# Decoder tables of a neural codec kernel: from scaled adds on ScalarE and VectorE to diagonal matmuls in PSUM

## The chip, the cores and the metric

The kernel runs on one core of a Trainium2 chip. The metric is the device time of one execution in microseconds. The engines are called PE (TensorE, matmuls), DVE (VectorE), ACT (ScalarE), POOL (GpSimd) and SP (SyncE, which only issues transfers here).

## The reference

The input x has shape (2, 16000, 512). A depthwise convolution of three taps along time, followed by SiLU, gives z. Four codebooks of eight vectors then quantise z one after another: each stage takes the nearest codebook vector and subtracts it. The sum of the chosen vectors goes through a second depthwise convolution of three taps.

```python
z = jnp.zeros_like(x)
for i in range(K):
    z = z + xp[:, i:i+T, :] * dw_enc[i][None, None, :]
z = _silu(z)
res = z
q = jnp.zeros_like(z)
for s in range(Nq):
    cb = codebooks[s]
    d2 = |res|^2 - 2.0 * res @ cb.T + |cb|^2
    sel = cb[d2.argmin(-1)]
    q = q + sel
    res = res - sel
for i in range(K):
    y = y + qp[:, i:i+T, :] * dw_dec[i][None, None, :]
```

All arrays are bf16; K is 3, Nq is 4, and the d2 line is shortened here.

## The kernel before

Each of the two sequences is cut into nine tiles, eighteen in all: the first sequence into 6, 8 and seven times 16 groups of 128 rows, the second into seven times 16, 8 and 6. A tile's rows are loaded transposed (channels on partitions) by DMA transposes from SP, one per group, into one of two XT buffers.

For each tile the steps are these. `front` makes the three taps (the "taps" steps, L531 on ACT or L532 on DVE, and adds through the helper at L364), then the exponential (L537) and one plus it (L538 or L539). `front2` takes the reciprocal (L549) and multiplies ("gate"). `select` computes inner products with codebooks on PE (L561, L567, "score0"), reads them on DVE (L601, L602), and decides the first three stages with small DVE steps ("decide"), small transposes copied to OT (L643 on ACT, L644 on DVE) and corrections on PE (L649). `windows` transposes the one-hot choices (L672) and copies them to OHW (L678, either engine). `resid` subtracts the chosen vectors: PE multiplies OHW by the negated codebook tables CBN (L701, with L700 adding Z through an identity where ACT evacuates), and ACT (L707) or DVE (L709) brings the result back to ZB. A second round of products and decisions (`score3`, `decide3`, `win3`) settles the last stage. `back` multiplies OHW by the decoder tables WDEC on PE (L758, L760, L762), ACT copies the result to YB (L766), and SP stores it (L789).

Because one one-hot window covers four neighbouring rows for every stage, a decoder table has 128 rows (stage, row offset jj, codeword) by 512 channels: row r holds the codebook vector (in CB4) times the decoder tap that belongs to the row offset jj of r. There are four tables WDEC[v]; v says which taps stand at which offsets, in `(0, 1, 2, None), (None, 0, 1, 2), (None, None, 0, None), (None, 2, None, None)`. JM[jj] is a column of ones and zeros that marks the partitions of offset jj. WDBC holds the three decoder taps, each repeated on all partitions; it lives in YB3, and the scratch rows WJ live in YB2. The negated stage tables CBN are made from CB4 in the same setup, and CB4 is copied from PSUM by ACT (L458).

In the kernel before, each table is a sum of terms tap times mask, made by ACT (L481) and added on DVE, and then one product with CB4 on DVE:

```python
add("ACT", 0.62, key, lambda t=t, k=k, jj=jj: nc.scalar.mul(t, WDBC[:, k, :], JM[jj]), [("Y", 3), ("JM", jj)], [("WJ", jj % 2)])
if acc is not None:
    tt(t, t, acc, ALU.add, 0.35, key, [("WJ", 1 - jj % 2)], [("WJ", jj % 2)])
...
tt(WDEC[v], CB4, acc, ALU.mult, 0.35, key, ["CB4", ("WJ", aj), ("Y", 3)], [("WDEC", v), ("Y", 2)])
```

The order of all instructions is made by a planner, class `Plan`. Every step is added with an engine, an assumed cost, a key and its dependences. `order` then replays the steps on assumed clocks: it always takes the step that can start earliest, and among equals the one of least rank. The rank comes from a table WHEN with three entries for each kind of step (the first three tiles, the middle, the last three). Steps that may run on two engines go to ACT only if it would end early enough by SLACK; evacuations of `resid` choose by SHARE. Where PE would idle long before a step that is not setup, the planner puts in filler matmuls (L809). The engines then execute their own instructions strictly in that order. Setup steps and the first tiles' steps are planned together, so setup work can lie between the first tiles' work.

Of the kernel before, what the change touches and what calls it, by code (L numbers as in the profile page):

```python
# [8 lines left out]
BF16 = mybir.dt.bfloat16  # L9
F32 = mybir.dt.float32  # L10
U16 = mybir.dt.uint16
ALU = mybir.AluOpType
# [4 lines left out]
class Plan:  # L17
# [9 lines left out]
    SPAN, BUSY = 3.413, 0.5  # L27
    GATE = {"resid": (1.0, 2.0), "back": (1.0, 2.0), "win0": (0.6, 1.5), "win3": (0.6, 1.5), "score0": (0.25, 1.4), "score3": (0.25, 1.4)}

    def __init__(self, pairs, edges, share, slack, quota, when):  # L30
        self.steps, self.writer, self.readers = [], {}, {}
        self.pairs, self.edges, self.share, self.slack, self.quota, self.when = pairs, edges, share, slack, quota, when

    def add(self, engine, cost, key, fn, reads=(), writes=(), take=None, free=None, hold=None, tail=0.0, after=(), dest=None, box=None, mm=0):
        n = len(self.steps)
        deps = set(after)
        for t in reads:
            if t in self.writer:
                deps.add(self.writer[t])
            self.readers.setdefault(t, []).append(n)  # L40
        for t in writes:
            if t in self.writer:
                deps.add(self.writer[t])
            deps.update(self.readers.get(t, ()))
            self.writer[t] = n
            self.readers[t] = []
        deps.discard(n)
        self.steps.append({"n": n, "e": engine, "c": cost, "k": key, "fn": fn, "deps": sorted(deps), "take": take, "free": free,
                           "hold": hold, "tail": tail, "dest": dest, "box": box, "mm": mm})
        return n  # L50
# [3 lines left out]

    def rank(self, s):
        w = self.when[s["k"][0]][self.part(s)]
        return w[0] + s["k"][1] + w[1] * s["k"][2]

    def product(self, t, c, share, half):

# [14 lines left out]
    def order(self):  # L75
# [17 lines left out]
        out = []  # L93
# [9 lines left out]
        def load(d, t):  # L103
            return max(clock[d] - t, 0.0) + held[d] + sum(cost(steps[m], d) for m in waiting[d]
                                                        if at[m] <= t + 1.0 and (d == "DVE" or not isinstance(steps[m]["e"], tuple)))
# [8 lines left out]
        def look(s, e):  # L114

            t = max(at[s["n"]], clock[e])
            if s["take"]:
                dest = s["dest"]
                if dest == "ANY":
                    full = [d for d in ("ACT", "DVE") if held[d] >= self.quota[d]]  # L120
                    if len(full) == 2:
                        return inf, None
                    if full:
                        dest = "ACT" if full[0] == "DVE" else "DVE"
                    else:
                        dest = "DVE" if load("DVE", t) + self.share[self.part(s)] < load("ACT", t) else "ACT"
                elif dest and held[dest] >= self.quota[dest]:
                    return inf, None
                kind = s["take"][0]
                t = place(kind[dest] if isinstance(kind, dict) else kind, t)[0]  # L130
                return t + late(many(s, dest), t, cost(s, dest) if s["dest"] == "ANY" else s["c"]), dest
            if isinstance(s["e"], tuple) and e == "ACT" and t + s["c"]["ACT"] > max(at[s["n"]], clock["DVE"]) + s["c"]["DVE"] + self.slack[self.part(s)]:
                return inf, None
            if s["mm"]:
                t += late(s["mm"], t, s["c"])
            return t, None
# [9 lines left out]
        while len(out) < len(steps):  # L146
# [38 lines left out]
                c += self.TABLE  # L185
            if s["mm"]:
                m = many(s, dest)
                c = self.product(t, c, *self.GATE.get(s["k"][0], (0.5, 1.5))) - t
                run += m
                if run > self.CHUNK:  # L190
                    run -= self.CHUNK
                    fetched = t + c * (m - run) / m + self.FETCH
# [4 lines left out]
            if s["free"]:  # L197
                if s["free"]["dest"]:
                    held[s["free"]["dest"]] -= 1
                for j in s["free"]["banks"]:  # L200
                    banks[j] = end + self.LATENCY[e]
            out.append(s)
            for u in users[n]:
                ue = steps[u]["e"]
                at[u] = max(at[u], t + c + self.AGAIN[e] if ue == e else end + self.LATENCY[e])
                left[u] -= 1
                if not left[u]:
                    open_(u)
# [5 lines left out]
def kernel(  # L214
# [27 lines left out]
    PAIR = 1  # L242
    NX, NE, NZ, NOH, NY = 2, 3, 4, 4, 4
    NA = 4
    SHARE = (19.5, 1.71, -1.34)
    SLACK = (0.8, -4.83, -5.72)
    QUOTA = {"ACT": 4, "DVE": 4}
    WHEN = {"setup": ((-0.05, 1.675), (0.613, 1.016), (0.464, 0.931)), "load": ((-2.074, 0.741), (-2.063, 0.601), (-2.58, 0.741)),
            "pad": ((-1.343, 0.11), (-1.736, 0.115), (-2.291, 0.134)), "taps": ((0.284, 0.643), (-0.413, 0.648), (0.441, 1.172)),
            "exp": ((0.672, 0.139), (0.624, 0.043), (0.853, 0)), "plus1": ((1.287, 0.521), (0.349, 0.234), (0.268, 0.646)),  # L250
            "recip": ((0.542, 0.819), (0.469, 0.213), (1.361, 0.627)), "gate": ((-0.104, 0.712), (0.552, 0.521), (1.523, 0.809)),
            "score0": ((-0.134, 0), (0.889, 0), (-0.19, 0)), "decide": ((1.83, 0.266), (-0.088, 0.293), (0.366, 0.69)),
            "win0": ((2.039, 0), (2.077, 0), (2.756, 0)), "resid": ((1.585, 0.742), (1.683, 0.632), (1.826, 0.993)),
            "score3": ((2.285, 1.086), (2.738, 0.327), (2.939, 1.624)), "decide3": ((1.327, 0.17), (2.815, 0.429), (3.624, 0.724)),
            "win3": ((3.135, 0.143), (3.003, 1.197), (2.818, 0.209)), "back": ((2.723, 0.576), (3.156, 1.159), (4.372, 0.628))}
    assert B == len(SIZES) and T >= GM * P and GM <= 16

    xf = x.flatten_outer_dims()
# [63 lines left out]
    CBN = {(s, u): sb([P, D], BF16, f"CBN{s}_{u}") for s in range(3) for u in range(2)}  # L322
    WDEC = [sb([P, D], BF16, f"WDEC{v}") for v in range(4)]

    plan = Plan(NA, (3, len(tiles) - 3), SHARE, SLACK, QUOTA, WHEN)
    add = plan.add

    def ps(box):
# [37 lines left out]
    def setup():  # L366
# [104 lines left out]
                       ["CB4", ("JN", u)], [("CBN", s, u)])  # L471

        key = ("setup", 2.3, 0)
        WJ = [YB[2][:, j, :] for j in range(2)]
        for v, tp in enumerate(((0, 1, 2, None), (None, 0, 1, 2), (None, None, 0, None), (None, 2, None, None))):
            acc = None
            for jj, k in enumerate(tp):
                if k is None:
                    continue
                t = WJ[jj % 2]  # L480
                add("ACT", 0.62, key, lambda t=t, k=k, jj=jj: nc.scalar.mul(t, WDBC[:, k, :], JM[jj]), [("Y", 3), ("JM", jj)], [("WJ", jj % 2)])  # L481
                if acc is not None:
                    tt(t, t, acc, ALU.add, 0.35, key, [("WJ", 1 - jj % 2)], [("WJ", jj % 2)])
                acc, aj = t, jj % 2
            tt(WDEC[v], CB4, acc, ALU.mult, 0.35, key, ["CB4", ("WJ", aj), ("Y", 3)], [("WDEC", v), ("Y", 2)])

    def load(st):
        n, G = st["n"], st["G"]
# [358 lines left out]
```

## Time and profile before

| quantity | value |
|---|---|
| median of 7 runs | 731.39 us (726.59 to 733.28) |
| profiled execution, its own time | 732.25 us |
| its span | 730.5 us |
| mean granted TensorE clock | 0.963 |
| time in the setup's eight ACT multiplies (L481) | 5.6 us in total |
| DMA, mean | 98 GB/s |

The span is the time from the first to the last recorded instruction of the profiled execution; its own time includes what lies around it. A row of a group names line, engine, operation, output and inputs with their shapes, how often, then the busy time in us and the mean of one in ns, then the idle time of the engine just before it and who ended it. Busy shares are averages over stages, so a table by stage is needed beside them.

### The profile page before, as it was taken

The page shows a single profiled execution, that of the slowest core. Times are in us where ns is not written, and L with a number is a line of the kernel's source. Part 1 is how long each engine was busy: PE and PEld are TensorE (multiplying, and loading weights), DVE is VectorE, ACT ScalarE, POOL GpSimd, SP SyncE. Part 2 cuts the span into 40 slices and gives each one's busy share as a digit, 9 for nine tenths or more (in the row PEclk, how much of TensorE's full clock was granted, in tenths as well). Part 3 has the DMA queues.
Part 4 walks back from the last instruction along what each step waited for, and adds up shares of the span by engine and source line. Part 5 has one row for each costly group of instructions (what it writes and reads, how often), then busy time and mean ns, then how long its engine had stood idle before and what let it go on. Part 6 is the DMA issues. An engine that isn't in the chain of part 4 may idle for free.

```text
span 730.5 us, 24317 instructions
## 1 busy us (share of the span) xinstructions
PE 584.9 (80%) x10656; PEld 289.4 (40%) x10725; DVE 675.2 (92%) x1258; ACT 658.5 (90%) x583; POOL 10.3 (1%) x35
## 2 busy tenths in 40 slices
PE   5977677886887887877788778877898797889995
PEld 2443243343443443434344333433444343444442
DVE  8779889999999999999998999999999999999993
ACT  6888988599999999899999999999899999999656
POOL 2000000000010000000000000000000010000000
PEclk9999798999999999999999999989999999999999
DMA  5444454534245343635534444442436151302316
GB/s 113 99 95 96 101 110 98 122 73 88 39 140 94 103 87 91 132 86 133 107 114 95 119 89 108 131 95 59 88 105 137 58 142 23 119 2 88 116 32 211
DMA packets 163968, 71.89 MB, mean 98 GB/s; under 512 B 155567, under 2 KB 155599, under 8 KB 163862
## 3 DMA queue, kind: packets, MB, share of 16 engines
q1 hardware_dynamic: 163646, 69.90, 40.0%
q8 instruction: 84, 1.38, 0.8%
q10 hardware_dynamic: 216, 0.43, 0.2%
q14 instruction: 22, 0.18, 0.1%
HBM read 0.43 MB, written 32.77 MB: 45 GB/s over the span
## 4 chain that ended last, share of the span: by engine, by line
DVE 51%; PE 27%; issue 8%; ACT 7%; SPq 3%; DMA 1%; DVEq 0%; ACTq 0%
DVE ZB L709 12%; PE ps L701 8%; DVE TA L364 7%; DVE TB L532 6%; PE ps L700 6%; DVE ZB L364 6%; PE ps L567 5%; SPq L493 3%; DVE TA L532 3%; PE ps L758 3%; DVE EX L539 2%; ACT YB L766 2%; DVE OHW L678 2%; PE ps L809 2%; ACT ZB L707 2%
## 5 line engine op out<-in xcount | busy, mean ns | idle before, releaser
L701 PE MATMUL ps<-OHW,CBN 128*128 128x512 bf16 (+1 forms) x768 | 267.4, 385 | 19.9 <-DVE ZB L709 10.7
L707 ACT CAST ZB<-ps 128x1024 bf16<-128x1024 f32 (+2 forms) x296 | 253.5, 931 | 32.0 <-PE ps L701 30.4
L700 PE MATMUL ps<-ZB,IDENT 128*128 128x512 bf16 (+1 forms) x530 | 204.9, 387 | 33.5 <-ACT ZB L707 14.1
L709 DVE TENSOR_TENSOR ZB<-ZB,ps 128x1024 bf16<-128x1024 bf16 (+2 forms) x136 | 143.1, 1064 | 4.0 <-PE ps L701 3.4
L766 ACT CAST YB<-ps 128x1024 bf16<-128x1024 f32 x126 | 121.8, 1042 | 11.1 <-PE ps L762 4.6
L701 PEld LDWEIGHTS <-CBN 128*128 128x128 bf16 x768 | 74.6, 99 | 142.8 <-issue 77.0
L537 ACT ACTIVATE EX<-ZB 128x4096 bf16<-128x4096 bf16 (+2 forms) x36 | 115.2, 3199 | 8.6 <-DVE ZB L364 8.3
L549 ACT ACTIVATE EX<-EX 128x4096 bf16<-128x4096 bf16 (+2 forms) x36 | 114.8, 3196 | 0.2
L567 PEld LDWEIGHTS <-ZB 128*32 128x32 bf16 x8064 | 75.3, 95 | 54.3 <-issue 51.1
L567 PE MATMUL ps<-ZB 128*32 128x64 bf16 x8064 | 87.3, 198 | 7.6 <-issue 4.6
L532 DVE TENSOR_SCALAR TB<-XT,WENC 128x2048 bf16<-128x2048 bf16 (+2 forms) x139 | 93.0, 688 | 0.2
L809 PE MATMUL ps<-MSK,IDENT 128*128 128x512 bf16 x277 | 71.5, 406 | 14.7 <-DVE RC L617 2.4
L758 PE MATMUL ps<-WDEC,OHW 128*128 128x512 bf16 x219 | 68.1, 388 | 14.1 <-DVE ZB L709 4.5
L700 PEld LDWEIGHTS <-IDENT 128*128 128x128 bf16 x530 | 52.6, 99 | 66.2 <-issue 13.8
L364 DVE TENSOR_TENSOR ZB<-ZB,EX 128x4096 bf16<-128x4096 bf16 (+2 forms) x36 | 72.7, 2021 | 3.7 <-ACT EX L549 3.6
L364 DVE TENSOR_TENSOR TA<-TA,TB 128x4096 bf16<-128x4096 bf16 (+2 forms) x36 | 72.8, 2021 | 1.0 <-ACT TB L531 0.6
L364 DVE TENSOR_TENSOR ZB<-TA,TB 128x4096 bf16<-128x4096 bf16 (+2 forms) x36 | 72.7, 2019 | 0.1
L809 PEld LDWEIGHTS <-IDENT 128*128 128x128 bf16 x294 | 29.0, 102 | 47.3 <-issue 19.9
L532 DVE TENSOR_SCALAR TA<-XT,WENC 128x2048 bf16<-128x2048 bf16 (+2 forms) x70 | 46.8, 688 | 0.9 <-DMA out_dram<-YB 0.4
L758 PEld LDWEIGHTS <-OHW 128*128 128x128 bf16 x252 | 22.9, 99 | 41.1 <-issue 18.4
L539 DVE TENSOR_SCALAR EX<-EX 128x4096 bf16<-128x4096 bf16 (+2 forms) x35 | 38.4, 1098 | 0.8 <-ACT EX L537 0.8
L678 DVE COPY OHW<-ps 96x1024 bf16<-96x1024 bf16 (+5 forms) x35 | 22.1, 631 | 10.1 <-PE ps L672 5.6
(100 smaller groups left out, 397.7 us busy)
## 6 DMA issues: line engine op xcount, KB each, us to landing
out_dram<-YB SPq DMA_DIRECT2D x33, 448.0 KB
out_dram<-YB SPq DMA_DIRECT2D x28, 512.0 KB
XT<-in_x_dram SPq DMA_TRANSPOSE x283
out_dram<-YB SPq DMA_DIRECT2D x30, 60.0 KB
out_dram<-YB SPq DMA_DIRECT2D x31, 2.0 KB
out_dram<-YB SPq DMA_DIRECT2D x2, 224.0 KB
YB<-in_dw_dec_dram ACTq DMA_DIRECT2D x1, 384.0 KB
out_dram<-YB SPq DMA_DIRECT2D x1, 384.0 KB
```

What stands on the lines that cost most here:

```text
L364: add("DVE", cost, key, lambda: nc.vector.tensor_tensor(out=out, in0=a, in1=b, op=op), reads, writes, **kw)
L532: lambda dst=dst, src=src, w=w: nc.vector.tensor_scalar(out=dst, in0=src, scalar1=w, scalar2=None, op0=ALU.mult),
L537: add("ACT", act(2 * R), ("exp", n, h), lambda: nc.scalar.activation(v(ex), Z, ACT.Exp, scale=-1.0), zt, [("EX", sl), "ACTTAB"], hold="E")
L549: nc.scalar.add_instruction(mybir.InstActivation(name=nc.get_next_instruction_name(), engine=mybir.EngineType.Activation, func=ACT.Reciprocal,
L567: nc.tensor.matmul(o[HB * q:HB * (q + 1), u * ZW:(u + 1) * ZW].rearrange("p (s c) -> p s c", s=2), lhsT=blk, rhs=both, start=False, stop=( ...
L700: nc.tensor.matmul(o, lhsT=IDENT, rhs=zg[:, k0:k0 + nk, :], start=True, stop=False)
L701: nc.tensor.matmul(o, lhsT=CBN[s, u][:, i * P:(i + 1) * P], rhs=W[:, k0:k0 + nk, PADC:PADC + P], start=not on_act, stop=True)
L707: nc.scalar.copy(zg, v)
L709: nc.vector.tensor_tensor(out=zg, in0=zg, in1=v, op=ALU.add)
L758: nc.tensor.matmul(o, lhsT=W[:, k, PADC:PADC + P], rhs=WDEC[u], start=True, stop=not wrap)
L766: add("ACT", act_psum(1024), key, lambda k=k, box=box, Y=Y, k0=k0: nc.scalar.copy(Y[:, 2 * (k - k0):2 * (k - k0) + 2, :].rearrange("p g d ...
L809: nc.tensor.matmul(PS[j // 2][:, 512 * (j % 2):512 * (j % 2) + NMK * ZW], lhsT=IDENT, rhs=MSK.rearrange("p u w -> p (u w)"), start=True, s ...
```

## The change

The terms are no longer built on ACT and DVE. Four diagonal matrices DJ[jj], the identity with only the rows of offset jj kept, are made on DVE. For each table PE multiplies them with the taps and sums the terms in one PSUM bank (three, three, one and one matmuls). DVE then multiplies CB4 with the sum straight from PSUM. The scratch rows in YB2 are no longer used. The planner's constants SHARE, SLACK and WHEN have other values, and it has new terms MARGIN and NUDGE, whose values here are neutral: zeros, a factor of one and an empty table.

```diff
-    SHARE = (19.5, 1.71, -1.34)
-    SLACK = (0.8, -4.83, -5.72)
+    SHARE = (18.22, 2.18, -1.48)
+    SLACK = (0.8, -4.91, -0.79)
     QUOTA = {"ACT": 4, "DVE": 4}
-    WHEN = {"setup": ((-0.05, 1.675), (0.613, 1.016), (0.464, 0.931)), "load": ((-2.074, 0.741), (-2.063, 0.601), (-2.58, 0.741)),
...
+    MARGIN = (0, 0, 0, 1)
+    WHEN = {"setup": ((0.01, 1.859), (0.613, 1.215), (0.919, 1.13)), "load": ((-1.633, 0.741), (-1.622, 0.601), (-2.139, 0.741)),
...
+    NUDGE = {}
...
-        WJ = [YB[2][:, j, :] for j in range(2)]
+        DJ = [sb([P, P], BF16, f"DJ{jj}") for jj in range(4)]
+        for jj in range(4):
+            add("DVE", 0.11, key, lambda jj=jj: nc.vector.tensor_scalar(out=DJ[jj], in0=IDENT, scalar1=JM[jj], scalar2=None, op0=ALU.mult),
+                [("JM", jj), "I"], [("DJ", jj)])
         for v, tp in enumerate(((0, 1, 2, None), (None, 0, 1, 2), (None, None, 0, None), (None, 2, None, None))):
-            acc = None
-            for jj, k in enumerate(tp):
...
-                add("ACT", 0.62, key, lambda t=t, k=k, jj=jj: nc.scalar.mul(t, WDBC[:, k, :], JM[jj]), [("Y", 3), ("JM", jj)], [("WJ", jj % 2)])
-                if acc is not None:
-                    tt(t, t, acc, ALU.add, 0.35, key, [("WJ", 1 - jj % 2)], [("WJ", jj % 2)])
-                acc, aj = t, jj % 2
-            tt(WDEC[v], CB4, acc, ALU.mult, 0.35, key, ["CB4", ("WJ", aj), ("Y", 3)], [("WDEC", v), ("Y", 2)])
+            use = [(jj, k) for jj, k in enumerate(tp) if k is not None]
+            bw = {}
+
+            def wmm(use=use, bw=bw):
+                for q, (jj, k) in enumerate(use):
+                    nc.tensor.matmul(ps(bw), lhsT=DJ[jj], rhs=WDBC[:, k, :], start=(q == 0), stop=(q == len(use) - 1))
+            j = add("PE", 0.43 * len(use), key, wmm, [("DJ", jj) for jj, _ in use] + [("Y", 3)], [], take=("S", bw), mm=len(use))
+            add("DVE", 0.6, key, lambda v=v, bw=bw: nc.vector.tensor_tensor(out=WDEC[v], in0=CB4, in1=ps(bw), op=ALU.mult), ["CB4"],
+                [("WDEC", v)], free=bw, after=[j])
```

The other WHEN entries change by small amounts, most by a few hundredths to a few tenths; the largest are "win3" of the last tiles (2.818 to 3.452) and "win0" of the last tiles (2.756 to 2.265). In the planner, `rank`, the choice of engine and the assumed ends of steps take the added MARGIN and NUDGE terms.

## The prediction

> **What bounds the kernel now.** I read the page's busy row first, then a table by stage, then the chain of work that ended last, then the groups by shape, and last who reads the tables.
>
> ```profile
> span 730.5 us, 24317 instructions
> PE 584.9 (80%) x10656; PEld 289.4 (40%) x10725; DVE 675.2 (92%) x1258; ACT 658.5 (90%) x583; POOL 10.3 (1%) x35
> ```
>
> VectorE (DVE) and ScalarE (ACT) are both near full. By stage (stretch in us, its length, then busy time and instructions of each engine, granted clock, DMA):
>
> ```profile
> 0.00:13.00 13.00, 5.11 (x23) 2.31 (x24) 10.34 (x60) 7.89 (x34) 3.78 (x29) 1.00 0.55 119
> 13.00:30.00 17.00, 16.95 (x75) 7.57 (x75) 13.10 (x29) 13.71 (x17) 0.00 (x0) 1.00 0.48 98
> 55.00:100.00 45.00, 31.00 (x470) 14.42 (x473) 38.66 (x57) 40.10 (x39) 0.00 (x0) 0.89 0.51 105
> 100.00:640.00 540.00, 435.46 (x8382) 217.23 (x8432) 518.11 (x871) 505.57 (x392) 6.52 (x6) 0.96 0.42 99
> 680.00:712.00 32.00, 29.85 (x620) 15.05 (x625) 30.20 (x78) 19.67 (x27) 0.00 (x0) 1.00 0.20 68
> ```
>
> From 100 to 640 us DVE is 96% busy and ACT 94%: this stretch pays only for less work or fewer waits. Before 30 us both have room (DVE 13.1 of 17), so there latency counts, not work. From 680 to 712 us DVE is 94% busy and ACT only 61%. The chain names what sets the early end (start, length, what):
>
> ```profile
> 20.41 2.80 DMA XT<-in_x_dram
> 23.24 0.71 ACT YB L481
> 23.96 1.28 ACT L549
> 25.29 1.36 issue
> 26.65 0.71 ACT YB L481
> 27.36 1.04 ACT TA L531
> ```
>
> Two of the removed multiplies (L481) stand in it; the tile-1 taps (L531) that end it had their data at 23.2. Earlier, in the timeline, two more stand before the codebook copy and the first taps:
>
> ```profile
> 8.09 0.72 ACT L481 ACTIVATE YB<-YB,JM 128x512 bf16<-128x512 bf16 x1 [1.74 <-DVE GREM L364]
> 8.72 0.57 ACT L458 CAST CB<-ps 128x512 bf16<-128x512 f32 x1
> 9.18 0.72 ACT L481 ACTIVATE YB<-YB,JM 128x512 bf16<-128x512 bf16 x1
> 10.22 0.61 POOL L504 COPY XT<-XT 128x508 bf16<-128x508 bf16 x1 [4.02 <-DMA XT<-in_x_dram]
> 12.56 0.94 ACT L531 ACTIVATE TA<-XT,WENC 128x768 bf16<-128x768 bf16 x1
> ```
>
> CB4's input left PE at 7.30 (6.70 + 0.60 for L456), yet the copy starts at 8.72, behind the first L481. The CBN products wait for it, and the tile-0 taps start at 12.56 although the edge copy that completes their data ended at 10.83.
>
> **The change part by part.**
>
> *ACT loses eight multiplies.*
>
> ```profile
> L481 ACT ACTIVATE YB<-YB,JM 128x512 bf16<-128x512 bf16 x8 | 5.6, 713 | 1.9 <-DVE GREM L364 1.7 <-DVE YB L364 0.2
> L364 DVE TENSOR_TENSOR WDEC<-CB,YB 128x512 bf16<-128x512 bf16 x4 | 1.7, 423 | 0.1
> L709 DVE TENSOR_TENSOR ZB<-ZB,ps 128x512 bf16<-128x512 bf16 x15 | 10.0, 683 | 0.1
> L758 PE MATMUL ps<-WDEC,OHW x219: 376/379/634, 66.6 to 722.4; 128*128 128x512 bf16 x110
> ```
>
> 8 x 0.713 = 5.7 us of ACT busy time go. Successive starts lie 0.61 to 0.63 apart, so 8 x 0.62 = 5.0 us of its line.
>
> *DVE swaps adds for PSUM products.* Out: four adds (0.42) and four products (0.423), 3.4 us. In: four products 128x512 with one source in PSUM. No such row exists; the SBUF row gives 0.42, L709's 128x512 form, with one source in PSUM too, 0.683. I take 0.683 as the nearer. In also: four DJ products 128x128. L532's rows (768 columns 0.417, 2048 0.75) give 0.26 ns a column, so an estimate of 0.25 at 128; the ends are 0.13 (JN, L464) and 0.29 (BD, 128x128 from f32). Together 4 x 0.683 + 4 x 0.25 = 3.7 us: DVE gets 0.3 us more, ends -1.2 and +0.5. I book 0: of its 17 us from 13 to 30, DVE has 3.9 free.
>
> *PE gets eight matmuls of 512 columns.* They fall where PE now runs fillers (L809). From 9.6 to 14.7 us twelve fillers took 5.04 us, 0.42 each, and from 14.7 to 20 us twenty-five took 5.25, 0.21 each, though the granted clock reads 1.00 in both. The Trainium skill, "TensorE: Matmul & The Clock Gate", Part 1, says the array starts at half rate until about 3.4 us of sustained work opens it, and falls back after an idle window of that length. By the first fillers the eight cost 3.4 us, by the granted clock column 1.7. Both are hidden, as the first real product of tile 0 starts at 30.8. But the rule speaks against the change in one place: the planner fills only from the last table matmul on, so a late table set would leave PE idle before it and score0 might run at half rate. 30 us of fillers shrinking to 10 would still be three windows, so I book 0. If that cover went, the first 96 products (0.9 us now) would take 1.8: +0.9.
>
> *Waits.* Each product waits for its matmuls and CB4; queued behind it on DVE are the taps and gate of tile 0. With PE idle after 9.7, the matmuls are done long before; bounds 0 and 4 x 0.4 = 1.6. I take 0. The tables hold at most four of the eight half tiles of PSUM, at a time when only setup wants any. YB2 and YB3 come free earlier, which nobody waits for before 69.7 us. The tables are read first at 66.6 us. No DMA is added.
>
> *What it is worth at the start.* Before the taps: ACT's line shortens by 8.72 - 7.30 = 1.4 and then by 0.6, 2.0 in all, but the data caps this at 12.56 - 10.83 = 1.7; DVE, which fills the gap with table products, gains less. I take 1.3. In the chain at 23.24 and 26.65: 2 x 0.6 = 1.2. Sum 2.5, ends 0 (DVE's products, at up to 0.6 apiece between starts, eat it) and 2.9. Does it last? Tile 2's last load leaves the queue at 46.1 and lands 2.8 later, at 48.9; its taps start at 51.9. So loads leave 3 us of room.
>
> *ACT's remaining room*: 5.0 - 2.0 - 1.2 = 1.8 us, enough for the planner to give one or two 768-column taps to ACT: 2 x 0.33 on DVE. -0.7, ends 0 and -0.7.
>
> *The planner's numbers.* MARGIN is (0, 0, 0, 1) and NUDGE empty, so the new terms add zero or multiply by one. SHARE, SLACK and WHEN change, and with them the whole order. Loads get ranks 0.44 tiles later, but still stand before any store ready at the same time; I book 0. SLACK's last entry, -5.72 to -0.79, lets ACT take copies and taps of the last three tiles. From 680 to 712 us DVE copies OHW (L678) for 0.34, 0.27 and 0.6 and OT for 0.13 twice, pitch each, 1.5 us, with ACT at 61%. I take -1.0, ends 0 and -1.5. For the 540 us between, the trace cannot show the new order: DVE idles 22 us there and ACT 34. Taking a fifth of DVE's idle as the stake, the bound is 4 either way, value 0.
>
> *Sum:* -2.5 - 0.7 - 1.0 = -4.2. The profiled execution took 732.25 (span 730.5 plus 1.75 around it), so 728.05. The median shown is 731.39, 0.86 lower: **727.2**, 0.57% faster. What a measurement here can tell from no change is about 0.5%, 3.66 us: faster below 727.7, slower above 735.0.
>
> **The rivals.**
>
> *A, the tables were hidden anyway.* They are needed only at 66.6 us, and DVE idles in the first 30. For it: in the timeline DVE waits 2.3 us for PE's products (L567) before 50.0, and 2.4 and 2.8 us for PE before 76.0 and 96.3, so an early lead can be spent at the next wait. Against: L481 in the chain itself. Time 731, spread 3 by the new order.
>
> *B, a cold PE in the new order (slower).* Around 73 to 94 us the granted clock is 0.72 to 0.79, matmuls in the chain follow each other at 0.43 us rather than 0.22, and DVE waits 2.4 us (L678) and 2.8 us (L601). One such stage costs 5.1 us. The reordered middle could open others; the planner predicts these windows from its own clock. One more makes 727.2 + 5.1 = 732.3; two make 737.4. It decides from about 1.5 such stages on (7.8 us).
>
> *C, the new weights find the idle time.* The middle gives the bound of 4 as well: 723.
>
> *The change not doing what it says* is small: the matmuls and products are written out; only their place is the planner's.
>
> **How the numbers follow.** Forecast 0.55 at 727.2, own range 722.5 to 731.5, of which 0.40 faster and 0.15 no change. A 0.20: 0.04, 0.12 and 0.04. B 0.20, slower. C 0.05, faster. Faster 0.49, same 0.27, slower 0.24. The range 721.5 to 737.5 takes in C with part of the start's upper end, and B up to its two-stage price; a tenth lies beyond each end.
>
> **What would show it.** Right: L481 gone, ACT's busy time down by 5 to 6 us; eight new PE matmuls of about 0.4 us pitch near 10 us; four DVE products near 0.68 from PSUM; tile-0 taps near 11.3 on ACT; tile-1 taps near 25 instead of 27.3; between 680 and 712 us more L678 on ACT. Wrong: the start two microseconds early but DVE's waits for PE from 55 to 640 us longer by more (then B), or tile-1 taps still past 27 (then A). DVE busy time up by over 1 us would break the product's price.

## The result, and the profile after

The median went from 731.02 us (31 runs, the seven of the table above among them) to 721.72 us (12 runs, 719.76 to 726.25): a ratio of 0.989 [0.9867, 0.9913], or 9.3 us faster. The forecast was 727.2, 4.2 us faster. The direction came as forecast; the forecast's size is less than half of what came. The profiled execution took 723.68 us, 8.57 less than the one of before, so the two traces show nearly all of the difference.

In the kernel after, the lines behind the change stand lower in the file: L482 makes the DJ, L490 is the table matmul and L492 the product. For the rest L364 became L370, L531 and L532 became L539 and L540, L537 L545, L549 L557, L567 L575, L678 L686, L700 and L701 L708 and L709, L707 and L709 L715 and L717, L809 L817.

The span and busy rows of the page after:

```profile
span 721.9 us, 24295 instructions
PE 580.8 (80%) x10652; PEld 289.1 (40%) x10729; DVE 670.1 (93%) x1252; ACT 658.6 (91%) x581; POOL 8.8 (1%) x35
```

ACT is as busy as before (658.5), although eight multiplies of 5.6 us are gone, and DVE is 5.1 us less busy (675.2). Something moved from DVE to ACT. The two largest rows of the page that can move, first of before and then of after:

```profile
L707 ACT CAST ZB<-ps 128x1024 bf16<-128x1024 f32 (+2 forms) x296 | 253.5, 931 | 32.0 <-PE ps L701 30.4
L709 DVE TENSOR_TENSOR ZB<-ZB,ps 128x1024 bf16<-128x1024 bf16 (+2 forms) x136 | 143.1, 1064 | 4.0 <-PE ps L701 3.4
```

```profile
L715 ACT CAST ZB<-ps 128x1024 bf16<-128x1024 f32 (+2 forms) x301 | 256.9, 939 | 28.8 <-PE ps L709 26.8
L717 DVE TENSOR_TENSOR ZB<-ZB,ps 128x1024 bf16<-128x1024 bf16 (+2 forms) x131 | 138.2, 1071 | 1.8 <-PE ps L709 1.0
```

Five of the 432 evacuations went from DVE to ACT: the last figures say that both engines also idle less in front of them. The table by stage of the kernel after, in the cuts of the prediction:

```profile
0.00:13.00 13.00, 5.61 (x26) 2.33 (x27) 10.51 (x62) 7.89 (x35) 3.78 (x29) 1.00 0.54 118
13.00:30.00 17.00, 14.43 (x130) 6.85 (x133) 12.21 (x23) 12.15 (x11) 0.00 (x0) 0.98 0.45 101
55.00:100.00 45.00, 30.52 (x444) 13.12 (x445) 38.75 (x60) 38.44 (x35) 0.00 (x0) 0.85 0.50 109
100.00:640.00 540.00, 439.62 (x8512) 221.89 (x8576) 521.81 (x899) 518.03 (x406) 5.02 (x6) 0.97 0.43 97
680.00:712.00 32.00, 29.88 (x624) 15.17 (x609) 26.33 (x78) 22.04 (x31) 0.00 (x0) 1.00 0.31 111
```

From 100 to 640 us DVE did 521.81 - 518.11 = 3.7 us more work and ACT 518.03 - 505.57 = 12.5 us more in the same time. The two share the work of the tiles, so half of the 16.2 us, 8.1 us, is an estimate of what this stretch ran ahead. It is nearly the whole difference of the executions, and it lies far from the tables, in the stretch for which the forecast booked nothing.

How a lead is read here, used below too: the DVE and ACT busy time still to come from a given moment is summed from the stages of each trace; the kernel that has less to come is ahead by half of the difference. Against the profile of before:

| kernel | 45 us | 100 | 200 | 300 | 400 | 500 | 600 | 680 |
|---|---|---|---|---|---|---|---|---|
| after | 0.6 | 0.0 | 2.8 | 2.8 | 4.6 | 5.2 | 8.0 | 7.5 |
| after, a second profile (t1) | 0.6 | 0.8 | 6.6 | 6.7 | 7.3 | 6.6 | 10.2 | 9.4 |
| before's order, new tables (e1) | 0.0 | 0.1 | 2.0 | 3.1 | 1.6 | 2.0 | 1.5 | 1.0 |
| after's order, old tables (e2) | -2.2 | -3.3 | 2.4 | 1.4 | 3.1 | 4.0 | 4.8 | 4.6 |

The two profiles of the one program differ by up to 3.9 us (at 300 us; 3.8 at 200), so a single entry is good to about that. The rows agree on this: after is about level with before at 100 us and some 8 to 10 us ahead at 600.

The groups of the new instructions in the first 30 us, in the trace after:

```profile
L490 PE MATMUL ps<-YB,DJ 128*128 128x512 bf16 x8 | 3.4, 579 | 1.3 <-DVE DJ L482 1.3
L492 DVE TENSOR_TENSOR WDEC<-CB,ps 128x512 bf16<-128x512 bf16 x4 | 2.7, 683 | 0.0
L482 DVE TENSOR_SCALAR DJ<-IDENT,JM 128x128 bf16<-128x128 bf16 x4 | 0.8, 243 | 0.0
```

The prices of the forecast hold: 0.683 us for a product (0.683 taken), 0.243 for a diagonal (0.25 taken).

### The profile page after: what moved, and what is told of

It reads as the page before. It is cut to its first block, busy times and chain, and to the rows that moved or that the text cites. A ratio compares the mean times of both kernels' runs of the same rounds, so it can differ in the third digit from the quotient of the medians.

```text
span 721.9 us, 24295 instructions
## 1 busy us (share of the span) xinstructions
PE 580.8 (80%) x10652; PEld 289.1 (40%) x10729; DVE 670.1 (93%) x1252; ACT 658.6 (91%) x581; POOL 8.8 (1%) x35
## 4 chain that ended last, share of the span: by engine, by line
DVE 52%; PE 24%; ACT 10%; issue 8%; SPq 3%; DMA 2%; DVEq 0%; ACTq 0%
DVE ZB L717 12%; DVE ZB L370 10%; PE ps L709 7%; PE ps L708 6%; DVE TB L540 6%; PE ps L575 4%; DVE TA L370 4%; ACT EX L545 3%; PE ps L817 3%; DVE EX L547 3%; DVE TA L540 3%; SPq L501 2%; DVE OHW L686 2%; ACT EX L557 2%; ACT ZB L715 2%
## 5 line engine op out<-in xcount | busy, mean ns | idle before, releaser
L715 ACT CAST ZB<-ps 128x1024 bf16<-128x1024 f32 (+2 forms) x301 | 256.9, 939 | 28.8 <-PE ps L709 26.8
L709 PE MATMUL ps<-OHW,CBN 128*128 128x512 bf16 (+1 forms) x768 | 265.6, 382 | 17.9 <-DVE ZB L717 9.6
L708 PE MATMUL ps<-ZB,IDENT 128*128 128x512 bf16 (+1 forms) x537 | 206.8, 385 | 30.5 <-DVE ZB L717 12.2
L717 DVE TENSOR_TENSOR ZB<-ZB,ps 128x1024 bf16<-128x1024 bf16 (+2 forms) x131 | 138.2, 1071 | 1.8 <-PE ps L709 1.0
L709 PEld LDWEIGHTS <-CBN 128*128 128x128 bf16 x768 | 74.6, 98 | 136.5 <-issue 68.8
L545 ACT ACTIVATE EX<-ZB 128x4096 bf16<-128x4096 bf16 (+2 forms) x36 | 115.0, 3198 | 10.4 <-DVE ZB L370 10.3
L557 ACT ACTIVATE EX<-EX 128x4096 bf16<-128x4096 bf16 (+2 forms) x36 | 114.7, 3196 | 0.7 <-DVE EX L547 0.5
L575 PE MATMUL ps<-ZB 128*32 128x64 bf16 x8064 | 88.7, 198 | 12.5 <-issue 5.6
L575 PEld LDWEIGHTS <-ZB 128*32 128x32 bf16 x8064 | 76.1, 96 | 53.3 <-issue 48.0
L540 DVE TENSOR_SCALAR TB<-XT,WENC 128x2048 bf16<-128x2048 bf16 (+2 forms) x135 | 90.9, 692 | 0.1
L817 PE MATMUL ps<-MSK,IDENT 128*128 128x512 bf16 x261 | 70.9, 415 | 13.4 <-issue 5.5
L708 PEld LDWEIGHTS <-IDENT 128*128 128x128 bf16 x537 | 53.1, 99 | 63.0 <-issue 9.5
L370 DVE TENSOR_TENSOR ZB<-ZB,EX 128x4096 bf16<-128x4096 bf16 (+2 forms) x36 | 72.7, 2019 | 3.6 <-ACT EX L557 3.5
L370 DVE TENSOR_TENSOR TA<-TA,TB 128x4096 bf16<-128x4096 bf16 (+2 forms) x36 | 72.8, 2022 | 1.2 <-ACT TB L539 0.8
L370 DVE TENSOR_TENSOR ZB<-TA,TB 128x4096 bf16<-128x4096 bf16 (+2 forms) x36 | 72.7, 2021 | 0.4
L540 DVE TENSOR_SCALAR TA<-XT,WENC 128x2048 bf16<-128x2048 bf16 (+2 forms) x71 | 48.3, 696 | 0.3
L817 PEld LDWEIGHTS <-IDENT 128*128 128x128 bf16 x283 | 27.9, 105 | 45.1 <-issue 21.4
L686 DVE COPY OHW<-ps 96x1024 bf16<-96x1024 bf16 (+5 forms) x34 | 21.7, 637 | 10.6 <-PE ps L680 6.8
```

What stands on the lines that cost most here:

```text
L370: add("DVE", cost, key, lambda: nc.vector.tensor_tensor(out=out, in0=a, in1=b, op=op), reads, writes, **kw)
L540: lambda dst=dst, src=src, w=w: nc.vector.tensor_scalar(out=dst, in0=src, scalar1=w, scalar2=None, op0=ALU.mult),
L545: add("ACT", act(2 * R), ("exp", n, h), lambda: nc.scalar.activation(v(ex), Z, ACT.Exp, scale=-1.0), zt, [("EX", sl), "ACTTAB"], hold="E")
L557: nc.scalar.add_instruction(mybir.InstActivation(name=nc.get_next_instruction_name(), engine=mybir.EngineType.Activation, func=ACT.Reciprocal,
L575: nc.tensor.matmul(o[HB * q:HB * (q + 1), u * ZW:(u + 1) * ZW].rearrange("p (s c) -> p s c", s=2), lhsT=blk, rhs=both, start=False, stop=( ...
L708: nc.tensor.matmul(o, lhsT=IDENT, rhs=zg[:, k0:k0 + nk, :], start=True, stop=False)
```

## The experiments

Two things changed at once: the table steps and the planner's numbers, and either one changes the order of the whole program. The experiments separate the steps, the order, and the numbers.

### The tables alone, the order held: e1 and e2

In e1 the order of before is kept instruction by instruction, and only the table steps are exchanged; to make room for the eight matmuls on PE, eight fillers fewer stand ahead of tile 0's products. In e2 the order of after is kept with the old table steps, and with eight fillers more. TAB holds the exchanged steps with the times at which the planner puts them, SKIP is the key of the steps left out. The core of e1 (e2 is its mirror image):

```diff
         for s in plan.order():
+            while TAB and s["t"] >= TAB[0][0]:
+                TAB.pop(0)[1]()
             if s["fill"]:
-                fill(*s["fill"])
-            s["fn"]()
+                fill(s["fill"][0], s["fill"][1] + (-8 if first else 0))
+                first = False
+            if s["k"] != SKIP:
+                s["fn"]()
```

> The order of before is kept instruction by instruction; only the table steps are exchanged: the multiplies, adds and products of before left out, the diagonal products, the eight matmuls and the four PSUM products put in at the planned times that the changed kernel gives them, and eight fillers fewer ahead of score0 of tile 0. Theory 'order' (the gain is that of a new order of everything, and the tables themselves are worth little): 728.5 to 731.5, since the tile-1 taps hardly moved in the profile after. Rival 'tables' (five microseconds off ACT are the gain): 721 to 725. The prediction's start term alone would be 728.5.

> The mirror: the order of the changed kernel kept, and the table steps of before put back at their own planned times, with eight fillers more. 'Order': 721.5 to 724. 'Tables': 728 to 731.

Measured: e1 731.55 us, ratio 0.9985 [0.9969, 1.0]; e2 725.75 us, ratio 0.9914 [0.9886, 0.9941]. So the tables alone are worth 0 to 0.3% in the order of before. The order of after, with the old tables, is worth 0.9%. What the tables add to it is the step from e2 to after, 0.9914 to 0.989, which the intervals don't separate: 1.8 us by the ratios, 4.0 by the medians. e2 came out between its two expected ranges, so neither theory holds alone. Most of the gain is the order's; in that order the tables may carry a part of it. In the table above e2 is 2.8 us behind after at 45 us and still 2.9 behind at 680.

The stages show the same split. From 100 to 200 us, in before, e1, e2 and after, in this order:

```profile
100.00:200.00 100.00, 79.63 (x1257) 38.81 (x1262) 94.53 (x165) 85.64 (x64) 0.00 (x0) 0.95 0.40 85
```

```profile
100.00:200.00 100.00, 81.52 (x1331) 40.49 (x1338) 95.89 (x167) 88.12 (x65) 0.00 (x0) 0.95 0.44 87
```

```profile
100.00:200.00 100.00, 75.98 (x1536) 38.77 (x1544) 96.64 (x160) 94.75 (x69) 0.00 (x0) 1.00 0.44 86
```

```profile
100.00:200.00 100.00, 79.33 (x1374) 39.67 (x1382) 94.33 (x156) 91.33 (x68) 0.00 (x0) 0.91 0.44 83
```

The fourth number after the length is ACT. In the order of before it works 86 to 88 of these 100 us, in the order of after 91 to 95, whichever tables the kernel has. The same holds for DVE from 300 to 400 us: 93.8 in before and 92.6 in e1, 97.0 in e2 and 97.2 in after.

### Numbers and step list exchanged: e3 and e4

In e3 the kernel after gets the three constants of before and plans anew; in e4 the kernel before gets those of after.

```diff
-    SHARE = (18.22, 2.18, -1.48)
-    SLACK = (0.8, -4.91, -0.79)
+    SHARE = (19.5, 1.71, -1.34)
+    SLACK = (0.8, -4.83, -5.72)
...
```

> The changed kernel with SHARE, SLACK and WHEN of before, planned anew. 'Order': the numbers fit only the list of steps they were set for, a handful of other steps in the setup shifts the whole order, so 733 to 742. 'Tables': 722 to 729, since the tables and not the numbers carry the gain.

> Before with SHARE, SLACK and WHEN of the changed kernel, planned anew. 'Order': 733 to 748. 'Tables': 729 to 733. If the new numbers are better in themselves, whatever the tables: 722 to 727.

Measured: e3 741.56 us, ratio 1.0128 [1.0101, 1.0156]; e4 750.03 us, ratio 1.0252 [1.0225, 1.028], 2 us above its expected range. Both are slower than either kernel. So neither set of numbers is the better one in itself: each belongs to its own list of steps. Twelve steps put in place of sixteen, with the numbers left alone, reorder the program and cost 10 us; the tables in a held order (e1) cost nothing. Had the change come without new numbers, it would have been slower.

### Where evacuations go: e5 and e6

After has 301 evacuations on ACT where before has 296. In e5 five of the middle ones of before go to ACT, in e6 five of after go to DVE, with the order otherwise kept.

```diff
+            if s["k"][0] == "resid" and s["take"] and (s["k"][1], round(s["k"][2] * 24)) in FLIP:
+                s["take"][1]["dest"] = "ACT"        # e6: "DVE"
             s["fn"]()
```

> Before, order kept, but one residual evacuation each of tiles 4, 6, 8, 10 and 12 goes from DVE (L709) to ACT (L707), with its identity matmul on PE. The changed kernel makes 301 evacuations on ACT and 131 on DVE where before made 296 and 136. Theory 'share' (five evacuations off DVE are the gain): 731 - 5 x 1.06 x about 0.7 = 726 to 729. Theory 'sequence' (the gain is fewer waits in a better sequence, and the count only follows): 730 to 735, since ACT is as full as DVE in the middle.

> The mirror: the changed kernel, order kept, five evacuations of the same tiles from ACT back to DVE. 'Share': 726 to 728. 'Sequence': 721 to 727, and not clearly more than what moving any five in a tuned order costs.

Measured: e5 733.93 us, ratio 1.0034 [1.0021, 1.0046]; e6 726.41 us, ratio 0.9929 [0.9902, 0.9957]. Moving five alone makes before slower and takes back three to five of after's eight to nine us (2.9 us by the ratios, 4.7 by the medians). In e5 the move itself did what it says:

```profile
PE 584.9 (80%) x10666; PEld 289.3 (39%) x10735; DVE 670.4 (91%) x1253; ACT 662.1 (90%) x588; POOL 8.5 (1%) x35
```

DVE's work falls from 675.2 to 670.4 us, to what after has, and the kernel is slower all the same. So the balance of the two engines alone is not the cause. e6 by itself decides nothing, since 726.41 lies in both of its expected ranges.

### The end: e7, e8 and t3

The forecast gave 1.0 us to copies of the last tiles that move to ACT. e7 puts five of them there in the order of before.

```diff
+            if s["box"] is not None and ((s["k"][0], s["k"][1]) in (("win0", 16), ("win0", 17), ("win3", 15)) or (s["k"][0] == "decide" and s["k"][1] == 17)):
+                s["box"]["dest"] = "ACT"
             s["fn"]()
```

> Before, order kept, but five copies of the last three tiles go from DVE to ACT: OHW of tiles 16 and 17 (stages 0 to 2), OHW of tile 15 (stage 3) and both OT copies of tile 17. It is the tail term of the prediction by itself: -1.0, so 729.5 to 730.5, if DVE at 94% is the bound between 680 and 712 us. If the chain of decisions there is bound by latency and not by DVE's load, ACT's longer copies make it no better or worse: 731 to 733.

Measured: 733.21 us, ratio 1.0008 [0.9996, 1.002]. No gain. After itself moved just one OHW copy off DVE (35 to 34 in the whole kernel), and none in the last tiles: from 680 to 712 us its trace has no OHW copy on ACT.

e8 is after with the numbers that before has for the last three tiles; its order is that of after until the planner's 483 us. t3 is its counterpart: before with the last numbers of after.

```diff
-    SHARE = (18.22, 2.18, -1.48)
-    SLACK = (0.8, -4.91, -0.79)
+    SHARE = (18.22, 2.18, -1.34)
+    SLACK = (0.8, -4.91, -5.72)
...
```

> The changed kernel with SHARE, SLACK and WHEN of the last three tiles as before; the planned order is the same up to the planned 483 us on SP and 581 us on DVE, and differs only after. If the last-tile numbers (SLACK -0.79) carry a part of the gain: 724 to 729. If the lead is earned in the middle and only kept at the end, as a comparison of the work left by time shows: 721 to 723.

> Before with only the last-tile numbers of the changed kernel; the planned order is the same up to the planned 485 us on SP and 585 us on DVE. If the new last numbers (SLACK -0.79 among them) are better in themselves: 727 to 729. If numbers and state fit each other only in pairs, as e8 suggests from the other side: 734 to 739.

Measured: e8 726.37 us, ratio 0.9931 [0.9899, 0.9964]; t3 736.72 us, ratio 1.0062 [1.0035, 1.0089]. The new last numbers keep about 4 us in the new order (3.0 by the ratios, 4.7 by the medians) and lose 4.5 in the old one. From 600 to 680 us, after and then e8:

```profile
600.00:680.00 80.00, 72.14 (x1362) 36.04 (x1373) 78.33 (x167) 74.52 (x70) 0.00 (x0) 1.00 0.20 68
```

```profile
600.00:680.00 80.00, 70.07 (x1328) 34.97 (x1336) 72.93 (x164) 71.68 (x67) 0.00 (x0) 0.98 0.21 74
```

DVE does 5.4 us less and ACT 2.8 us less in these 80 us in e8, half of it 4.1: e8's lead falls there from 10.4 to 5.8. So the end does matter, but in the 80 us ahead of the copies that the forecast pointed at, and with both engines busier there, not by copies moved to ACT.

### The first tiles' numbers alone: s3

After, with the new numbers for the first three tiles and those of before from then on.

```diff
-    SHARE = (18.22, 2.18, -1.48)
-    SLACK = (0.8, -4.91, -0.79)
+    SHARE = (18.22, 1.71, -1.34)
+    SLACK = (0.8, -4.83, -5.72)
...
```

> New tables, SHARE, SLACK and WHEN of the first three tiles as in the changed kernel, of all later tiles as before, planned anew. If the numbers of the first tiles carry the gain: 722 to 727. If the middle's numbers do: 731 to 742, with the lead at 100 us still that of the changed kernel.

Measured: 730.41 us, ratio 0.9976 [0.9961, 0.9991], between the two expected ranges. With e8 this gives a ladder of ratios: 0.9976 with the new first numbers, 0.9931 with the middle ones too, 0.989 with all. The steps are not independent, though. The trace of s3 leads by 6.8 us at 600, against 8.0 in after, and by 2.6 at 680: it too loses its 4 us from 600 to 680, as e8 does. By this one profile, within the 3.9 us that two profiles of one program can differ, the old middle numbers are as good up to 600 us.

### The start: r11, s1 and s2

The forecast's start fell short, as the next section shows: from 13 to 22 us DVE has no room for the PSUM products. r11 is after with three of the four products held back until DVE waits for tile 0's reciprocal; s1 is the same in e1's order; s2 holds back all four.

```diff
+            if s["k"] == ("setup", 2.3, 0) and s["on"] == "DVE" and s["t"] > 12:
+                held.append(s["fn"])
+                continue
             s["fn"]()
+            for _ in range({last["taps"]: 2, last["plus1"]: 1}.get(s["n"], 0)):
+                held.pop(0)()
```

> The changed kernel, order kept, but three of the four PSUM products leave DVE's dense stretch from 13 to 17 us and run where DVE waits for the reciprocal of tile 0, near 22 to 26 us. Theory (the start failed because the products lie on DVE's line, 8.8 us busy of 9 there, and not ACT's): tile 0's and tile 1's steps come 1.0 to 1.8 us earlier, 720 to 721.5. If a lead at the start is lost at the next wait: 721.5 to 723.

> The order of before with the new tables, and three of the four products in DVE's wait for the reciprocal, as in r11. Theory (the table change fails at the start only because of where its products stand): 0.75 us earlier at the gate of tile 0, as r11's profile shows, and 1 to 3 us at the end: 728 to 730. If r11's gain belongs to the new order alone: 731 to 732, as e1.

> The changed kernel with all four products in DVE's wait, the first one, at 10.39 in the profile after, too. It held back the copies of ACT behind it (RP) by 0.5 us. If that reaches the end: 718 to 719. If tile 0's first taps are bound by ACT's small copies and the data: 719 to 720, as r11.

In s2 the last table is read from a PSUM bank that another table's matmuls have filled again: WDEC[3] has other values, and the work is the same in kind and count.

Measured: r11 719.22 us, ratio 0.9846 [0.9823, 0.9868]; s1 730.92 us, 0.9983 [0.9966, 1.0001]; s2 720.94 us, 0.9846 [0.9819, 0.9872], above both of its ranges and no better than r11. From 13 to 22 us, before, after and r11:

```profile
13.00:22.00 9.00, 8.95 (x38) 3.96 (x38) 8.92 (x21) 5.74 (x10) 0.00 (x0) 1.00 0.44 98
```

```profile
13.00:22.00 9.00, 8.95 (x42) 4.09 (x42) 8.82 (x18) 4.45 (x5) 0.00 (x0) 1.00 0.43 97
```

```profile
13.00:22.00 9.00, 8.95 (x37) 3.87 (x37) 8.24 (x18) 4.83 (x6) 0.00 (x0) 1.00 0.43 98
```

The number after the two of PE is DVE's: it fills 8.8 to 8.9 of the 9 us in both kernels and 8.2 in r11. What that is worth at tile 0's gate (the product of ZB and EX) is counted from the first tile-0 taps on ACT, since these start between 12.2 and 12.9 us in the profiles of after and r11. The timeline of r11:

```profile
12.20 0.94 ACT L539 ACTIVATE TA<-XT,WENC 128x768 bf16<-128x768 bf16 x1
...
21.38 1.28 DVE L492 TENSOR_TENSOR WDEC<-CB,ps 128x512 bf16<-128x512 bf16 x2
...
25.81 0.96 DVE L370 TENSOR_TENSOR ZB<-ZB,EX 128x1536 bf16<-128x1536 bf16 x1 [1.64 <-ACT EX L557]
```

25.81 - 12.20 = 13.6 us, and 13.6 in its second profile (t2); after took 14.2 and 14.4. So the gap is worth 0.6 to 0.8 us at the gate. In s1 the same distance is 13.0 against 14.1 in e1, a full us, and the time is that of e1 (0.9983 and 0.9985): a us won before 27 us is lost again in the order of before. In the order of after the ratio fell from 0.989 to 0.9846. r11 came out below its expected range, and its 2.5 us are more than the 0.6 to 0.8 us at the gate; where the rest is won was not settled. That pair was run once more, on one chip, as told below.

### The fillers: r9, r10 and r12

Fillers stand in the chain of waits of after, for instance:

```profile
71.29 5.28 PE ps L817 x12
...
136.94 6.63 PE ps L817 x19
```

r9 is after without the fillers that the planner places after its first 60 us, r10 the same in before, r12 is after with half of them.

```diff
-            if s["fill"]:
+            if s["fill"] and s["t"] < 60:                                         # r9, r10
                 fill(*s["fill"])
...
-                fill(*s["fill"])
+                fill(s["fill"][0], s["fill"][1] if s["t"] < 60 else s["fill"][1] // 2)   # r12
```

> The changed kernel, order kept, without the filler matmuls (L817) planned after 60 us. They stand in the chain with 5.28 us at 71.29 and 6.63 us at 136.94. If they only delay the transposes behind them: 714 to 720. If they keep PE at full clock and that is worth more than they cost: 724 to 732.

> Before, order kept, without the fillers (L809) planned after 60 us; in its chain they have 2.34 us at 73.04, 2.25 at 118.7 and 5.74 at 131.25. Theory 'sequence': the distance between the two kernels does not come from fillers, so this stays 7 to 10 us above the changed kernel without them. If fillers in the chain were the difference between 100 and 200 us: it comes 3 us nearer.

> The changed kernel with each run of fillers after 60 us cut to half. Between the two cases of no late fillers: 718 to 722 if they mostly delay, 722 to 728 if the clock is worth more.

Measured: r9 726.71 us, ratio 0.994 [0.9918, 0.9963], granted clock 0.933 against 0.962; r10 731.94, 1.0022 [1.0001, 1.0042], clock 0.929 against 0.963; r12 730.76, 0.999 [0.9973, 1.0008]. The late fillers are worth 3.7 us to after by the ratios (5.0 by the medians) and 1.6 (1.0) to before. So a part of after's lead rests on them, a quarter by the ratios and under a half by the medians: r10 was expected to stay 7 to 10 us above r9 if the distance did not come from fillers, and stands 0.8%, 5 to 6 us, above it. The rest of the lead is there without them. r12 fell outside both of its ranges, and is taken up at the end.

### After and r11 once more: t1 and t2

t1 is the program of after, unchanged, and t2 that of r11, on one chip.

> The changed kernel unaltered, beside the next two on one chip: 720.5 to 723. It gives the distance of r11 from it directly, and shows how far the work left by time differs between two profiles of one program.

> r11 once more beside the changed kernel: 718.5 to 720.5, 2 to 3 us below it, if moving three products out of DVE's dense stretch is worth what r11 showed; level with it, 721 to 723, if r11 was favoured by its chip.

Measured: t1 721.56 us, ratio 0.987 [0.9843, 0.9896]; t2 719.82 us, ratio 0.9847 [0.9816, 0.9878]. t2 is 1.7 us below t1, less than the 2 to 3 expected, and r11 2.5 below the median of after: the same sign twice, with intervals that overlap in this pair. r11 is the version with the lowest time here: about 2 us below after, and 1.5% below before in each of its two runs.

## Why the forecast was right in direction and wrong in size

**The step that failed: the middle, booked at 0 within 4.** Of the terms that the forecast did book, the start brought about 0.5 us at tile 0's gate and the other two nothing that can be seen; the gain came from the term that it set at 0. That the direction was right was therefore luck. The forecast said that the trace cannot show the new order, and took a fifth of DVE's 22 us of idle time as the stake. In place of it the order brought most of the gain (e2 against before: 0.9914). The stake was cut too small, in two ways that can be worked out afterwards. It left out ACT's idle, 34 us, though ACT and DVE share the evacuations, taps and copies; and it is ACT that filled up, by 12.5 us. And by the engines' sum the stake was 22 + 34 = 56 us, halved 28; a fifth of that is 5.6, and the 8.1 that came are 29% of it. Rival C, which let the new weights find idle time and was priced with the same bound at 723, was nearest, at a chance of 0.05.

Where in the middle? The stretches that repeat in both profiles of after are 100 to 200 us (ACT 85.6 in before; 91.3 and 94.0), 300 to 400 (DVE 93.8; 97.2 and 95.9) and 500 to 600 us. The last of them, before, after and t1:

```profile
500.00:600.00 100.00, 83.14 (x1788) 42.00 (x1801) 94.78 (x152) 93.53 (x78) 2.05 (x2) 0.95 0.41 105
```

```profile
500.00:600.00 100.00, 80.94 (x1608) 40.51 (x1608) 97.34 (x166) 96.57 (x75) 0.72 (x2) 0.98 0.43 105
```

```profile
500.00:600.00 100.00, 82.97 (x1588) 41.20 (x1586) 97.70 (x169) 97.91 (x76) 0.72 (x2) 0.98 0.43 99
```

One long wait can be named, but it is not the cause. From 100 to 200 us, the first row below is the longest of ACT's waits in before, the second the longest in after and in t1 (what waited, for what, sum, times, longest):

```profile
ACT OT L643 <- PE ps L639: 6.8, 1, 6.8
```

```profile
ACT EX L545 <- DVE ZB L370: 4.7, 1, 4.7
```

In before ACT stood still for 6.8 us in front of one small copy of transposed decisions, which waited for a transpose on PE behind 19 fillers:

```profile
131.25 5.74 PE L809 MATMUL ps<-MSK,IDENT 128*128 128x512 bf16 x19 [1.99 <-DVE S L602]
136.83 0.22 PE L639 MATMUL ps<-IDENT,OHA 128*128 128x128 bf16 x1
```

The 2.1 us between the two waits would be 1 us of lead, since the lead counts by halves. But the order of before has this wait at 2.7 us in r10, where those fillers are gone, and at 4.8 in e1, and neither kernel is clearly faster than before (1.0022 and 0.9985). Which waits, which of the new numbers or which exchange of two steps make the new order better was not settled. e3, e4 and t3 show that no set of numbers does so by itself, and s3 that the old middle numbers reach about the same lead at 600 us. It is open.

**The start, booked at -2.5, came out at 0.2 in this pair of profiles, and at about 0.5 over eleven.** Two of its readings were right. The codebook copy starts at 7.70 instead of 8.72. And the eight table matmuls are hidden; PE's timeline has seven of them in one row,

```profile
9.89 2.82 PE L490 MATMUL ps<-YB,DJ 128*128 128x512 bf16 x7
```

0.40 each, as the fillers of that time had suggested and not the clock column, which would have made them half as long. But the lead did not last. The first tile-0 taps on ACT start at 12.32 (forecast 11.3; before 12.56): the small copies that stood in front of them in ACT's queue still do, and the first of these (RP) now waits until 11.10 for the first PSUM product on DVE. From there to the gate of tile 0 the kernel after takes 26.56 - 12.32 = 14.24 us, and before took 26.78 - 12.56 = 14.22. And the tile-1 taps start at 27.43 (forecast 25):

```profile
26.56 0.96 DVE L370 TENSOR_TENSOR ZB<-ZB,EX 128x1536 bf16<-128x1536 bf16 x1 [2.24 <-ACT EX L557]
27.43 0.88 DVE L540 TENSOR_SCALAR TA<-XT,WENC 128x1024 bf16<-128x1024 bf16 x2
```

The step that failed inside this term is the sentence that DVE has 3.9 us free of the 17 from 13 to 30 us. That is a mean over two halves: from 13 to 22 us DVE was full, 8.92 of 9, and the free time lay behind 22. The chain showed ACT, but DVE was hardly earlier. Three products went into the full half, 0.6 us each from start to start, ahead of the sum that ends the first half's taps (ZB<-TA,TB). After, and then before:

```profile
13.87 0.68 DVE L492 TENSOR_TENSOR WDEC<-CB,ps 128x512 bf16<-128x512 bf16 x1
14.46 0.95 DVE L370 TENSOR_TENSOR TA<-TA,TB 128x1536 bf16<-128x1536 bf16 x1
15.33 0.68 DVE L492 TENSOR_TENSOR WDEC<-CB,ps 128x512 bf16<-128x512 bf16 x1
15.93 0.42 DVE L540 TENSOR_SCALAR TB<-XT,WENC 128x768 bf16<-128x768 bf16 x1
16.26 0.69 DVE L492 TENSOR_TENSOR WDEC<-CB,ps 128x512 bf16<-128x512 bf16 x1
16.86 0.95 DVE L370 TENSOR_TENSOR ZB<-TA,TB 128x1536 bf16<-128x1536 bf16 x1
```

```profile
15.00 0.42 DVE L364 TENSOR_TENSOR YB<-YB 128x512 bf16<-128x512 bf16 x1
15.33 0.42 DVE L532 TENSOR_SCALAR TB<-XT,WENC 128x768 bf16<-128x768 bf16 x1
15.66 0.42 DVE L364 TENSOR_TENSOR WDEC<-CB,YB 128x512 bf16<-128x512 bf16 x1
16.09 0.96 DVE L364 TENSOR_TENSOR ZB<-TA,TB 128x1536 bf16<-128x1536 bf16 x1
```

In before two steps of the old tables stood there, an add and a product, some 0.75 us together. Three times 0.6 less 0.75 is the 1.0 us by which this sum now comes later after the first taps (16.86 - 12.32 = 4.5 us, before 16.09 - 12.56 = 3.5). ACT, freed of its multiplies, waits for DVE instead: in e1, where the order is that of before, the second exponential of tile 0 waits 3.54 us for ZB, where it waited 2.27 in before. The forecast had named this as the lower end of the term ("DVE's products, at up to 0.6 apiece between starts, eat it") and held it for the less likely. r11 shows it from the other side, with the products in DVE's gap and the gate 0.6 to 0.8 us earlier.

One execution of each kernel hides a part of the term. Five profiles have the start of before (before, e5, e7, r10, t3) and six that of after (after, t1, e6, e8, r9, r12), since their edits act later. In the five the first tile-0 taps start at 12.6 to 13.9 us and the gate at 26.8 to 28.0, mean 27.5; in the six at 12.2 to 12.9 and 26.6 to 27.3, mean 26.9. What moves in the five is the first multiply, with the codebook copy queued behind it on ACT: it starts at 8.1 to 9.4 us, and the first taps 4.5 us after it in each. In e7 and t3 it waits for the decoder taps from the DMA; e7:

```profile
9.38 0.72 ACT L481 ACTIVATE YB<-YB,JM 128x512 bf16<-128x512 bf16 x1 [2.86 <-DMA YB<-in_dw_dec_dram]
10.01 0.56 ACT L458 CAST CB<-ps 128x512 bf16<-128x512 f32 x1
```

In before, the earliest, these start at 8.09 and 8.72. The change takes the multiply, and with it this wait, out of ACT's queue, which the forecast could not see in its one trace. By the reading of leads, e7 and t3 are 1.2 and 1.5 us behind before at 45 us, and 0.1 and 0.8 at 200: in that order part of such a distance is gone by then.

For the tables alone rival A was therefore right in the order of before, by e1 and s1: what is won before 30 us is spent at later waits. It was wrong for the whole, since it took the new order for a spread of 3 us.

**ACT's remaining room, booked at -0.7,** was used as the forecast said: of the 768-column taps DVE makes 8 in the first 60 us instead of 10, and ACT 4 instead of 2. But it bought nothing that can be seen; DVE's line was taken up by the products. Over the whole kernel ACT's 5.6 us were filled again, five evacuations among it, and e5 shows that such a shift is worth nothing alone.

**The last tiles, booked at -1.0,** failed as a mechanism: e7 shows no gain of it, and after has no OHW copy on ACT from 680 to 712 us. The new last numbers are worth 4 us in the new order, through 600 to 680 us (e8), which was not in the sum.

**Rival B, a cold PE in the new order,** did not come at its price. The granted clock is 0.85 from 55 to 100 us, against 0.89 before, and the chain of after has two filler stretches of 5.3 and 6.6 us; but from 100 to 640 us the clock is 0.97 against 0.96, and the whole is faster. The forecast's cover was over-counted: the fillers ahead of tile 0 last 21 us in before (from 9.66 to 30.8), not 30, and 14 in after. The one place where the clock rule was said to speak against the change did show once: the 88 later products of tile 0's score at 29.23 us took 1.36 us, where before took 0.89. These two us in after and in t1, the same program:

```profile
29.00:31.00 2.00, 1.44 (x89) 1.40 (x91) 1.17 (x2) 0.98 (x1) 0.00 (x0) 0.57 0.89 90
```

```profile
29.00:31.00 2.00, 1.08 (x90) 0.92 (x91) 1.17 (x2) 1.66 (x2) 0.00 (x0) 1.00 0.87 131
```

The clock is 0.57 in one and 1.00 in the other, so this 0.5 us comes and goes between executions of one program, and it shows in no lead: both are 0.6 ahead at 45 us. In after, PE did 0.24 us of work in the 2.8 us from 26.47 to 29.23; in t1 the same work stood in 1.8 us (28.12 to 29.92), and in r9, with 2.7 us, the clock was 0.79 and the products took 0.99. The page "TensorE: Matmul & The Clock Gate" of the Trainium skill (Part 1) says that the clock falls after at least one idle window of about 3.4 us, and that this window runs freely, so that the moment of the change varies from run to run. Here less than such a window was enough, and the traces don't separate the moment from the length of the stretch. The forecast's +0.9 was about twice what it cost when it came.

## What to carry to other kernels

Where a change to a few steps goes through a planner, it is two changes, the steps and the order, and a forecast has to price both: here the steps were worth 0 to 0.3% in the old order held, a new order 0.9%, and the same steps under unfitted numbers cost 1.3%. As the stake of a new order, count the idle time of all engines that can take each other's work, not that of the busiest one alone; what share of it an order wins (here 29%) is not known ahead. Room on an engine is read in the stretch where the new instruction will stand: a mean over 17 us hid that its first 9 were full. And one trace is one execution: here the gate of the first tile stood up to 1.2 us apart in profiles with the same start.

## What the runs showed of the hardware that was not expected

- Half of the late fillers is worse than none: ratios to before of 0.999 for r12, 0.994 for r9, 0.989 with all. The mean granted clock was 0.933 without, 0.951 with half and 0.962 with all, so the clock alone does not tell the order of the times. Why half of them costs more than none was not settled.
- Two profiles of one program, 2 us apart at the end, can be 3.9 us apart in lead at 300 us. A single trace's stage is no evidence for a cause below that.
- An idle stretch of PE of 2.8 us with 0.24 us of work in it was followed by a granted clock of 0.57 over the next two microseconds in one execution; one of 1.8 us in another execution of the same program by 1.00, and one of 2.7 us in r9 by 0.79.
- The first multiply of the tables started between 8.09 and 9.38 us in the five profiles with the start of before. In the two latest the trace shows it waiting for the decoder taps from the DMA, and what was queued behind it on ACT moved with it.
